# Attention and a gated block on one core: in the first four slots, where the weights' half-made words stand, when their passes come, and who copies block C

## The chip, the cores and the metric

The kernel runs on one core of one Trainium2 chip. The metric is the device time of one execution, in microseconds (us). Inputs are in the chip's main memory; the host only lays data out.

## The reference, cut to what matters

```python
# attention: q, k, v are (8, 8, 576, 64); blocks of 64 positions, block-causal mask
scores = (q @ k.T) / sqrt(64)                     # per batch and head
scores = where(block(i) >= block(j), scores, -1e9)
attn = exp(scores - max(scores))
attn = attn / (sum(attn) + 1e-9)
x = (attn @ v)                                    # heads joined: (8, 576, 512)
# gated block
h = gelu_tanh(x @ w_in)                           # w_in (512, 1024)
u, v = h[..., :512], h[..., 512:]
v_n = (v - mean(v)) / sqrt(var(v) + 1e-6) * g_ln  # over the last axis
v_s = w_sg @ v_n + b_sg                           # w_sg (576, 576), over positions
out = x + (u * v_s) @ w_out                       # w_out (512, 512)
```

w_in and w_out come as 64-bit floating-point words; everything else is 32-bit. The products keep nearly full 32-bit accuracy: each operand is split into a high and a low part (`hi`, `lo`) of a type that TensorE multiplies at speed, and three products are added up.

## The kernel before, in words

The attention is done for pairs of heads: 8 batches x 4 pairs = 32 pairs, one pair in one *slot* of the main loop (slots 0 to 31). Slots 0 to 3 are the first batch and run `opening_slot`; the others run `slot`, where pieces of the gated block of the batch before are put between the steps. This text is about slots 0 to 3.

A pair's 576 query rows are five blocks of rows: number 0 has 64 rows, numbers 1 to 4 have 128. Under the mask, block i has 64 + 128 i columns (64, 192, 320, 448, 576). Its work is spread over two slots. In slot n:

- TensorE turns the exponents of pair n (in `prob0` to `prob4`) by transposes, in five groups of four 128x128 tiles, each group in one PSUM bank: A0 and A1 (row block 4, first and second head), B0 and B1 (row blocks 3 and 1), C (row block 2, both heads). The banks are named `pA`, `pB`, `pC`; each is copied to SBUF into `ptA`, `ptB`, `ptC`. The table `TE` says which engine copies: ScalarE A0 and B0, VectorE A1, B1 and C.
- VectorE makes the inverse sums (`r`), ScalarE spreads them (`rx`).
- TensorE makes the first score products `s` of pair n+1 (row blocks 4, 1 and 0), then `turn_sums`: transposes of the diagonal blocks and of `rx` into banks `pd` and `pe`, which ScalarE copies to `rb`.
- VectorE adds the mask to the scores and takes their maxima in one custom instruction (`prob<-s,mask`, and a short one that reads the accumulator, `negm`): the *first maxima*. The one for row block 1 writes `prob1`, which the transposes for `pd` still read, and so waits for them. ScalarE then makes the exponents with their sums (`prob<-prob,negm`).
- `second` does the same for row blocks 3 and 2: the *second products, maxima and exponents*.
- `products`: TensorE multiplies the turned exponents by `v` into bank `ob` (a last piece goes to `pe`); `normalise`: VectorE multiplies `ob` by `rb` into `x`, which is spilled to memory. The high and low parts `xh` and `xl` are made in the next slot (`split_pending`).
- `split_qk`: GpSimd splits q and k of pair n+2 into `qh`, `ql`, `kh`, `kl`, one buffer each, so that it has to wait until the second products of pair n+1 have read the old ones.

The weights w_in come in 256 columns at a time and need work, since they are 64-bit words. `Double` takes a raw tile apart: ScalarE makes one word from the high halves (`m`), and three VectorE instructions, the *passes* of `single`, make the 32-bit number: one takes three bits from the low halves, one adds the sign, one adds `m`. The words `raw`, `m` and `t` all are in SBUF pages of the tag `w`. GpSimd then splits the number into `wi_h` and `wi_l` (`split_weight`). The generator `load_weight` gives these three steps one by one, and each call of `weight_half` takes one; the eight tiles of part "v" are treated three, two, two and one at a time in slots 0 to 3, and parts "u", "s" (the spatial matrix) and "o" come in later slots.

PSUM has eight banks, all of one pool (`bank`); a new tile takes a bank that its last user has left. Up to slot 3 VectorE, ScalarE and GpSimd do their instructions in the order in which the code writes them; from slot 4 on only TensorE does, and a scheduler places the others. Transfers are issued by SyncE in one queue: an issue that waits holds up those behind it.

Of the kernel before, what the change touches and what calls it, by code (L numbers as in the profile page):

```python
# [9 lines left out]
F32 = mybir.dt.float32  # L10
F32R = mybir.dt.float32r
BF16 = mybir.dt.bfloat16
U32 = mybir.dt.uint32
AF = mybir.ActivationFunctionType
ALU = mybir.AluOpType
# [5 lines left out]
def kernel(  # L21
# [13 lines left out]
    B, H, D, S = qT.shape  # L35
    P = 128
    BLK = 64
    DM = H * D
    DFF = w_in.shape[1]
    DH = DFF // 2  # L40
# [11 lines left out]
    class Engine:  # L52


        def __init__(self, letter, engine):
            self.letter, self.engine = letter, engine
# [5 lines left out]
    vector = Engine("V", nc.vector)  # L62
# [13 lines left out]
    def page(dtype, n, name):  # L76
        tag, bufs = KINDS.get(name, KINDS["w"])
        return sp.tile([P, n], dtype, tag=tag, name=name, bufs=bufs)

    def bank(name):  # L80
        return psum.tile([P, 512], F32, tag="bank", name=name, bufs=8)
# [7 lines left out]
    def turn(out, in_):  # L89
        return tensor.transpose(out, in_, ident)  # L90

    def copy(e, dst, src):
        f = {"v": vector.tensor_copy, "a": scalar.copy, "g": gpsimd.tensor_copy}[e]
        return f(dst, src)
# [3 lines left out]
    raw = {}  # L98
# [13 lines left out]
    def split_qk(n):  # L112
        out = []
        for x, t in zip(raw.pop(n), "qk"):
            hi = sp.tile([P, S], F32R, tag=t + "h", name=t + "h", bufs=1)
            lo = sp.tile([P, S], F32R, tag=t + "l", name=t + "l", bufs=1)
            if n == 0:
                copy("v" if t == "q" else "a", hi, x)
                vector.tensor_tensor(lo, x, hi.bitcast(F32), op=ALU.subtract)
            else:  # L120
                copy("g", hi, x)
                behind["G"] = gpsimd.tensor_tensor(lo, x, hi.bitcast(F32), op=ALU.subtract)
            out += [hi, lo]
        qk[n] = out

    def load_v(n):
        b, h = PAIRS[n]
        v_f, v_d = vals[n] = v_bufs[n % 2]
        lo, hi = slice(0, BLK), slice(BLK, P)
        for a, r in ((0, lo), (1, hi)):  # L130
            cols = slice((h + a) * D, (h + a + 1) * D)
            x = v[b, : (NT - 1) * P, cols].rearrange("(j p) d -> p j d", p=P)
            if a == 0:
                nc.sync.dma_start(v_f[:, :, r], x)
            else:
                nc.sync.dma_start(v_f[lo, :, r], x[hi])
                nc.sync.dma_start(v_f[hi, :, r], x[lo])
            nc.sync.dma_start(v_d[r, : NT - 1, r], x[lo])
            nc.sync.dma_start(v_d[r, NT - 1, r], v[b, S - TAIL :, cols])
# [24 lines left out]
    for s in (0, 1):  # L164
        t = cp.tile([P, NT - 1, 2 * D], F32, name=f"v_f{s}")
# [11 lines left out]
    wi_h = cp.tile([P, NC, DFF], F32R, name="wi_h")  # L177
    wi_l = cp.tile([P, NC, DFF], F32R, name="wi_l")
    wo_h = cp.tile([P, NC, DM], F32R, name="wo_h")
    wo_l = cp.tile([P, NC, DM], F32R, name="wo_l")  # L180
# [5 lines left out]
    def split_weight(x, dh, dl):  # L186
        gpsimd.tensor_copy(dh, x)
        gpsimd.tensor_tensor(dl, x, dh.bitcast(F32), op=ALU.subtract)

    class Double:  # L190


        def __init__(self, raw, name):
            n = raw.shape[-1]
            words = raw.bitcast(U32).rearrange("p (n t) -> p n t", t=2)
            self.hi, self.lo = words[:, :, 1], words[:, :, 0]
            tm = page(U32, 2 * n, name)
            self.t, self.m = tm[:, :n], tm[:, n:]
            scalar.activation(
                self.m.bitcast(F32), self.hi.bitcast(F32), AF.Abs, scale=2.0**-112  # L200
            )

        def single(self):
            t = self.t
            vector.tensor_scalar(t, self.lo, 29, None, op0=ALU.logical_shift_right)
            vector.scalar_tensor_tensor(
                t, self.hi, 0x80000000, t, op0=ALU.bitwise_and, op1=ALU.bitwise_or
            )
            vector.scalar_tensor_tensor(
                t, self.m, 3, t, op0=ALU.logical_shift_left, op1=ALU.bitwise_or  # L210
            )
            return t.bitcast(F32)

    def load_weight(src, cols, dh, dl, name="w", ahead=2, groups=()):

        W = 256
        parts = [(c, slice(f, f + W)) for f in range(cols.start, cols.stop, W) for c in range(NC)]
        raws = {}

        def fetch(k):  # L220
            if k < len(parts):
                c, fs = parts[k]
                raws[k] = page(src.dtype, W, name)
                nc.sync.dma_start(raws[k], src[c * P : (c + 1) * P, fs])

        for k in range(ahead):
            fetch(k)
        k = 0
        for size in (*groups, *([1] * len(parts))):
            if k == len(parts):  # L230
                return
            opened = []
            for j in range(k, k + size):
                fetch(j + ahead)
                raw = raws.pop(j)
                opened.append(raw if src.dtype == F32 else Double(raw, name))
            yield False
            if src.dtype != F32:
                opened = [x.single() for x in opened]
            yield False  # L240
            for j, x in zip(range(k, k + size), opened):
                c, fs = parts[j]
                split_weight(x, dh[:, c, fs], dl[:, c, fs])
            k += size
            yield True

    def load_spatial():
# [20 lines left out]
        for j in range(NT - 1):  # L268
# [15 lines left out]

    weights = deque(
        [
            ("v", load_weight(w_in, slice(DH, DFF), wi_h, wi_l, "w", 3, (3, 2, 2, 1))),
            ("u", load_weight(w_in, slice(0, DH), wi_h, wi_l)),
            ("s", load_spatial()),
            ("o", load_weight(w_out, slice(0, DM), wo_h, wo_l, "xr", 0)),  # L290
        ]
    )

    def weight_half():

        while weights:
            said = next(weights[0][1], None)
            if said is not None:
                return said
            weights.popleft()  # L300
# [16 lines left out]
    class Scores:  # L317
# [85 lines left out]
        def second(self):  # L403
            self.step((3, 0, EXT[3]))
            self.step((2, 0, EXT[2]))

    TE = {"A0": "a", "A1": "v", "B0": "a", "B1": "v", "C": "v"}
    PLACES = {
        "A0": [(0, 4, j) for j in range(4)],
# [6 lines left out]
    class Values:  # L416
# [9 lines left out]
        def turn(self, which):  # L426

            t = bank("p" + which)
            pt = sp.tile([P, 512], F32, tag="pt", name="pt" + which, bufs=5)
            for c, (a, i, j) in enumerate(PLACES[which]):  # L430
                c = slice(c * P, (c + 1) * P)
                k = BLK + P * (i - 1 - j) if a else P * j
                turn(t[:, c], prob[a][i][:, k : k + P])
                self.pt[a, i, j] = pt[:, c]
            copy(TE[which], pt, t)

        def inverse(self):

# [270 lines left out]
    def load_share(n, k):  # L709

        if n in WS:
            with ExitStack() as order:
                for ins in behind.values():
                    order.enter_context(tc.issue_after(ins.ins))
                for _ in range(WS[n][k]):
                    weight_step()

    PLAN = ["1112", "2114", "2114", "2114"]
    FIRST = ["1112", "1111", "1111", "2114"]
    Q = H // 2  # L720

    def split_pending():

        for f in pending:
            f()
        pending.clear()

    def opening_slot(n, va):

        va.turn("A0")  # L730
        va.turn("A1")
        va.turn("B0")
        va.turn("B1")
        va.inverse()
        split_pending()
        va.turn("C")
        load_v(n + 1)
        load_qk(n + 2)
        nx = Scores(n + 1)
        for p in nx.FIRST:  # L740
            nx.products(*p)
        va.turn_sums()
        weight_half()
        for p in nx.FIRST:
            nx.softmax(*p)
        weight_half()
        if n < Q - 1:
            nx.second()
            split_qk(n + 2)
            weight_half()  # L750
            va.products()
            va.normalise()
            pending.append(va.split)
        else:
            weight_half()
            va.products()
            va.normalise()
            va.split()
            nx.second()
        nv = Values(n + 1, nx)  # L760
        if n == Q - 1:
            nv.inverse()
            split_qk(n + 2)
        return nx, nv

    def slot(n, va):
        nx = n + 1 < N
        k = 6 if n // Q == 1 else 3
        g = [int(x) for x in (FIRST if n // Q == 1 else PLAN)[n % Q]]
        if n + 1 < N:  # L770
# [25 lines left out]
        load_share(n, 2)  # L796
        if n == Q + 1:
            run_side(2 * NT + 1)
        if n % Q == Q - 1:
            va.split()  # L800
# [81 lines left out]
```

## Time and profile before

| what | value |
|---|---|
| median of 3 runs | 758.80 us (758.28 to 758.92) |
| the profiled execution's own time | 758.84 us |
| its span in the profile | 757.0 us |
| mean granted TensorE clock | 0.993 |
| TensorE busy | 735.8 us (97%) |
| VectorE busy | 474.8 us (63%) |
| ScalarE busy | 425.3 us (56%) |
| GpSimd busy | 305.0 us (40%) |

The profile calls the engines PE (TensorE's matmuls and transposes), DVE (VectorE), ACT (ScalarE), POOL (GpSimd) and SP (SyncE, whose queue issues transfers). The span is from the first to the last instruction. Shares are means over the whole span: a stage with other limits has to be read by itself. In rows in order of time the first number is the start in us from the span's start and the second the length; a bracket gives the idle time of the engine just before and what ended it. A row that ends in "x2" stands for two instructions that follow each other. Line 60 is the helper that records nearly all instructions, so rows are told apart by the names of their tiles.

### The profile page before, as it was taken

To read this page: it belongs to the slowest core of one execution; us is meant where nothing else is said; L and a number is where in the kernel's file an instruction comes from. 1 tells how busy PE (TensorE), PEld (TensorE's weight loads), DVE (VectorE), ACT (ScalarE), POOL (GpSimd) and SP (SyncE) were. 2 spreads that over 40 slices of the span, in tenths; PEclk is the share of its full clock that TensorE was granted. 3 is DMA by queue.
4 is the path that set the end of the run, shared out by engine and by line. 5 is a ranking of instruction groups with operands and counts; after the bars stand their busy time and mean duration, and the time that the engine had idled before them with its cause. 6 is when DMAs were issued, how large, how long until landed. Compare 5 with 4: busy or idle time off the path is not lost.

```text
span 757.0 us, 18446 instructions
## 1 busy us (share of the span) xinstructions
PE 735.8 (97%) x6946; PEld 693.2 (92%) x6946; DVE 474.8 (63%) x1477; ACT 425.3 (56%) x1064; POOL 305.0 (40%) x376
## 2 busy tenths in 40 slices
PE   8779998999999999999999999999999999999998
PEld 7668998989899899999999899998999989998998
DVE  6988889765855359544785348664495645941732
ACT  5666767457744678337764377544873467721600
POOL 3755697634445323343433334351234532322121
PEclk9979999999999999999999999999999999999999
DMA  6626243333352223322234122521235221120032
GB/s 195 199 69 213 68 121 98 85 95 93 105 160 71 58 79 95 108 69 71 71 118 118 32 71 70 175 75 48 58 85 163 71 57 54 65 78 16 2 126 94
DMA packets 84300, 70.05 MB, mean 93 GB/s; under 512 B 59890, under 2 KB 59890, under 8 KB 84212
## 3 DMA queue, kind: packets, MB, share of 16 engines
q1 hardware_dynamic: 84212, 68.88, 31.0%
q8 instruction: 55, 0.90, 0.5%
q14 instruction: 33, 0.27, 0.1%
HBM read 49.98 MB, written 18.87 MB: 91 GB/s over the span
## 4 chain that ended last, share of the span: by engine, by line
PE 73%; DVE 8%; POOL 5%; DMA 5%; ACT 3%; issue 3%; SPq 2%; DVEq 0%; POOLq 0%; ACTq 0%
PE accs L60 16%; PE acco L60 11%; PE accv L60 11%; PE accu L60 9%; PE s L60 8%; PE ob L60 8%; PE pB L60 3%; PE pA L60 2%; PE pd L60 2%; DVE w L60 2%; ACT prob L60 2%; DVE prob L60 2%; DMA xr<-in_w_out 1%; PE pC L60 1%; POOL rs L60 1%
## 5 line engine op out<-in xcount | busy, mean ns | idle before, releaser
L60 ACT ACTIVATE prob<-prob,negm 128x576 f32<-128x576 f32 (+3 forms) x320 | 176.6, 554 | 70.1 <-DVE negm L60 68.9
L60 DVE CUSTOM_DVE_ANT_0 prob<-s,mask 128x256 f32<-128x256 f32 (+3 forms) x320 | 119.8, 418 | 44.9 <-PE s L60 41.6
L60 POOL TENSOR_TENSOR xh<-x,xh 128x64 fp32r<-128x64 f32 x32 | 10.8, 337 | 196.2 <-DVE xh L60 174.4
L60 POOL TENSOR_TENSOR gl<-u,gh 128x288 fp32r<-128x288 f32 x64 | 52.1, 819 | 88.7 <-DVE gh L60 72.8
L60 PE MATMUL acco<-gh,wo_h 128*128 128x288 f32 x256 | 77.6, 303 | 1.7 <-ACT ptB L60 1.4
L60 PE MATMUL accu<-xh,wi_h 128*128 128x288 f32 x256 | 78.3, 306 | 0.3 <-DVE negm L60 0.3
L60 PE MATMUL accs<-ws_h,vh 128*128 128x288 f32 x256 | 78.0, 305 | 0.0
L60 PE MATMUL accs<-ws_h,vl 128*128 128x288 f32 x256 | 75.5, 295 | 1.7 <-DVE vl L60 1.7
L60 PE MATMUL acco<-gl,wo_h 128*128 128x288 f32 x256 | 75.5, 295 | 0.0
L60 PE MATMUL accu<-xl,wi_h 128*128 128x288 f32 x256 | 75.5, 295 | 0.0
L60 PE MATMUL accs<-ws_l,vh 128*128 128x288 f32 x256 | 75.4, 295 | 0.0
L60 PE MATMUL accu<-xh,wi_l 128*128 128x288 f32 x256 | 75.3, 294 | 0.0
L60 PE MATMUL acco<-gh,wo_l 128*128 128x288 f32 x256 | 75.3, 294 | 0.0
L60 DVE TENSOR_TENSOR u<-accs,u 128x288 f32<-128x288 f32 x64 | 29.2, 457 | 58.3 <-PE accs L60 57.4
L60 PE MATMUL accv<-wi_h,xh 128*128 128x512 f32 x160 | 65.4, 409 | 0.0
L60 PE MATMUL s<-kh,qh 64*128 64x320 f32 (+4 forms) x384 | 64.2, 328 | 0.0
L60 PE MATMUL accv<-wi_l,xh 128*128 128x512 f32 x160 | 62.9, 393 | 0.0
L60 PE MATMUL s<-kh,ql 64*128 64x320 f32 (+4 forms) x384 | 59.8, 305 | 0.9 <-POOL ql L60 0.9
L60 ACT ACTIVATION_READ_ACCUMULATOR prob<-prob,negm 128x1 f32 x320 | 60.0, 188 | 0.0
L60 PE MATMUL s<-kl,qh 64*128 64x320 f32 (+4 forms) x384 | 58.8, 304 | 0.3 <-POOL kl L60 0.3
L60 ACT COPY vv<-accv 128x512 f32<-128x512 f32 x32 | 18.6, 581 | 65.6 <-PE accv L60 65.6
L60 PEld LDWEIGHTS acco<-gh,wo_h 128*128 128x128 f32 x256 | 48.1, 188 | 3.4 <-ACT ptB L60 1.8
(115 smaller groups left out, 2088.5 us busy)
## 6 DMA issues: line engine op xcount, KB each, us to landing
q_f<-in_qT SPq DMA_DIRECT2D x32, 288.0 KB, 3.1
k_f<-in_kT SPq DMA_DIRECT2D x32, 288.0 KB, 3.1
spill<-x SPq DMA_DIRECT2D x32, 288.0 KB, 2.7
xr<-spill SPq DMA_DIRECT2D x32, 288.0 KB, 3.0
out_T<-xr SPq DMA_DIRECT2D x32, 288.0 KB, 2.8
v_f<-in_v SPq DMA_DIRECT2D x32, 128.0 KB, 2.6
v_d<-in_v SPq DMA_DIRECT2D x64, 64.0 KB, 2.7
v_f<-in_v SPq DMA_DIRECT2D x64, 64.0 KB, 2.6
```

What stands on the lines that cost most here:

```text
L60: return lambda *a, **k: pin(method(*a, **k), self.letter)
```

## The change

Three edits, all in effect in slots 0 to 3 alone.

1. For part "v" the first two passes write their half-made word into a PSUM bank (`bank("w")`); the third reads it there and writes the finished number to SBUF.
2. In slots 0, 1 and 2 the call of `weight_half` that makes the passes moves behind `nx.second()`. Slot 3 keeps its order.
3. Block C of pairs 0 to 3 is copied by ScalarE.

```diff
     class Double:
-        def __init__(self, raw, name):
+        def __init__(self, raw, name, part):
             n = raw.shape[-1]
+            self.part = part
...
         def single(self):
-            t = self.t
-            vector.tensor_scalar(t, self.lo, 29, None, op0=ALU.logical_shift_right)
+            t = x = self.t
+            if self.part == "v":
+                x = bank("w").bitcast(U32)[:, : t.shape[-1]]
+            vector.tensor_scalar(x, self.lo, 29, None, op0=ALU.logical_shift_right)
             vector.scalar_tensor_tensor(
-                t, self.hi, 0x80000000, t, op0=ALU.bitwise_and, op1=ALU.bitwise_or
+                x, self.hi, 0x80000000, x, op0=ALU.bitwise_and, op1=ALU.bitwise_or
             )
             vector.scalar_tensor_tensor(
-                t, self.m, 3, t, op0=ALU.logical_shift_left, op1=ALU.bitwise_or
+                t, self.m, 3, x, op0=ALU.logical_shift_left, op1=ALU.bitwise_or
             )
...
+    Q = H // 2
     TE = {"A0": "a", "A1": "v", "B0": "a", "B1": "v", "C": "v"}
...
-            copy(TE[which], pt, t)
+            copy("a" if which == "C" and self.n < Q else TE[which], pt, t)
...
         for p in nx.FIRST:
             nx.softmax(*p)
-        weight_half()
         if n < Q - 1:
             nx.second()
+            weight_half()
             split_qk(n + 2)
             weight_half()
             va.products()
             va.normalise()
             pending.append(va.split)
         else:
+            weight_half()
             weight_half()
             va.products()
```

(The calls of `load_weight` pass the part's name.)

On VectorE, in slot 1, from the last of the first maxima (row block 0, 64x64) to the copy of A1, before:

```order
L60 ISA prob_110,negm<-s,mask 64x64
L60 ISA negm 64x1
L60 TENSOR_SCALAR w<-w 128x256
L60 SCALAR_TENSOR_TENSOR w<-w 128x256 x2
L60 TENSOR_SCALAR w<-w 128x256
L60 SCALAR_TENSOR_TENSOR w<-w 128x256 x2
L60 ISA prob_113,negm<-s,mask 128x448
L60 ISA negm 128x1
L60 ISA prob_113,negm<-s,mask 128x7x64
L60 ISA negm 128x1
```

and now:

```order
L60 ISA prob_113,negm<-s,mask 128x448
L60 ISA negm 128x1
L60 ISA prob_113,negm<-s,mask 128x7x64
L60 ISA negm 128x1
L60 ISA prob_112,negm<-s,mask 128x320
L60 ISA negm 128x1
L60 ISA prob_112,negm<-s,mask 128x5x64
L60 ISA negm 128x1
L60 TENSOR_SCALAR w<-w 128x256
L60 SCALAR_TENSOR_TENSOR w<-w 128x256 x2
L60 TENSOR_SCALAR w<-w 128x256
L60 SCALAR_TENSOR_TENSOR w<-w 128x256 x2
```

The two weights' passes (`w<-w`) stood ahead of the four second maxima (prob_113 is row block 3, prob_112 row block 2) and now stand behind them, ahead of normalise.

On ScalarE, from the copy of A0 to the weights' step, in slot 1 before:

```order
L60 COPY ptA_452<-pA_451 128x512
L60 COPY ptB_466<-pB_465 128x512
L60 COPY rx<-r 128x640
L60 COPY rb<-pd 128x512
L60 COPY rb<-pe 128x384
L60 ACTIVATE w<-w 128x256 x2
```

and now:

```order
L60 COPY ptA_455<-pA_454 128x512
L60 COPY ptB_469<-pB_468 128x512
L60 COPY rx<-r 128x640
L60 COPY ptC<-pC 128x512
L60 COPY rb<-pd 128x512
L60 COPY rb<-pe 128x384
L60 ACTIVATE w<-w 128x256 x2
```

The copy of block C came in, behind rx. On VectorE it is gone from behind `xh<-x`.

In SyncE's queue, the loads that are issued in slot 1 and 2 (pair 3's v, the spill, pair 4's q and k), before:

```order
L138 DMA v_d_107<-in_v 64x4x64
L490 DMA spill<-x 128x576
L136 DMA v_f_106<-in_v 64x4x64
L137 DMA v_f_106<-in_v 64x4x64
L138 DMA v_d_107<-in_v 64x4x64
L109 DMA k_f<-in_kT 128x576
```

and now:

```order
L227 DMA w<-in_w_in 128x256
L108 DMA q_f<-in_qT 128x576
L139 DMA v_d_107<-in_v 64x64 x2
L109 DMA k_f<-in_kT 128x576
L134 DMA v_f_106<-in_v 128x4x64
L138 DMA v_d_107<-in_v 64x4x64
L494 DMA spill<-x 128x576
L136 DMA v_f_106<-in_v 64x4x64
L137 DMA v_f_106<-in_v 64x4x64
L138 DMA v_d_107<-in_v 64x4x64
```

The loads of q and k stand ahead of most of the v loads and of the spill. TensorE's order is the same instruction by instruction through the whole program. From slot 4 on the scheduler changed little: in one place, near 120 us of the profile before, VectorE now makes all four low parts `vl` of the gated block ahead of a pair's normalise, where two stood behind it.

More of the change, by code (lines that the diff above doesn't have):

```diff
@@ L203, in single, with load_weight @@
         def single(self):
-            t = self.t
-            vector.tensor_scalar(t, self.lo, 29, None, op0=ALU.logical_shift_right)
+            t = x = self.t
+            if self.part == "v":
+                x = bank("w").bitcast(U32)[:, : t.shape[-1]]
+            vector.tensor_scalar(x, self.lo, 29, None, op0=ALU.logical_shift_right)
             vector.scalar_tensor_tensor(
-                t, self.hi, 0x80000000, t, op0=ALU.bitwise_and, op1=ALU.bitwise_or
+                x, self.hi, 0x80000000, x, op0=ALU.bitwise_and, op1=ALU.bitwise_or
             )
             vector.scalar_tensor_tensor(
-                t, self.m, 3, t, op0=ALU.logical_shift_left, op1=ALU.bitwise_or
+                t, self.m, 3, x, op0=ALU.logical_shift_left, op1=ALU.bitwise_or
             )
             return t.bitcast(F32)
-    def load_weight(src, cols, dh, dl, name="w", ahead=2, groups=()):
+    def load_weight(part, src, cols, dh, dl, name="w", ahead=2, groups=()):
         W = 256
@@ L235, in load_weight @@
                 raw = raws.pop(j)
-                opened.append(raw if src.dtype == F32 else Double(raw, name))
+                opened.append(raw if src.dtype == F32 else Double(raw, name, part))
             yield False
@@ L286 @@
         [
-            ("v", load_weight(w_in, slice(DH, DFF), wi_h, wi_l, "w", 3, (3, 2, 2, 1))),
-            ("u", load_weight(w_in, slice(0, DH), wi_h, wi_l)),
+            ("v", load_weight("v", w_in, slice(DH, DFF), wi_h, wi_l, "w", 3, (3, 2, 2, 1))),
+            ("u", load_weight("u", w_in, slice(0, DH), wi_h, wi_l)),
             ("s", load_spatial()),
-            ("o", load_weight(w_out, slice(0, DM), wo_h, wo_l, "xr", 0)),
+            ("o", load_weight("o", w_out, slice(0, DM), wo_h, wo_l, "xr", 0)),
         ]
@@ L719 @@
     FIRST = ["1112", "1111", "1111", "2114"]
-    Q = H // 2
     def split_pending():
```

## The prediction

> **What bounds the kernel now.** I read the page's head first, then the busy time by stage, then what TensorE waits for, the chain of waits, and last each engine's order of time in the first four slots. On the page:
>
> ```profile
> PE 735.8 (97%) x6946; PEld 693.2 (92%) x6946; DVE 474.8 (63%) x1477; ACT 425.3 (56%) x1064; POOL 305.0 (40%) x376
> ```
>
> TensorE sets the end. By stage (from:to, length, then busy us of PE, PEld, DVE, ACT, POOL, PE's clock, DMA share, GB/s):
>
> ```profile
> 24.20:39.10 14.90, 10.36 (x126) 8.63 (x126) 14.30 (x41) 8.86 (x28) 14.26 (x20) 0.96 0.48 137
> 39.10:54.30 15.20, 12.16 (x127) 11.07 (x127) 12.96 (x41) 8.92 (x28) 8.63 (x12) 0.81 0.27 73
> 140.00:757.00 617.00, 611.47 (x5659) 580.63 (x5657) 358.67 (x1121) 329.58 (x803) 215.79 (x253) 1.00 0.29 84
> ```
>
> Late in the span TensorE is 99% busy; in slots 1 and 2 it is not, while VectorE and GpSimd are nearly full. The waits of PE (total, times, longest; first row before 64 us, the others behind it), and from the chain of waits the rows of slot 1 (start, length):
>
> ```profile
> PE pB L60 <- ACT prob L60: 9.1, 4, 4.1
> PE accs L60 <- DVE vl L60: 1.7, 1, 1.7
> PE pA L60 <- ACT vh L60: 1.1, 1, 1.1
> ```
>
> ```profile
> 35.55 1.59 DVE w L60
> ...
> 38.30 0.50 ACT prob L60
> ...
> 39.12 1.97 PE pB L60 x8
> ```
>
> So in a slot TensorE's block B waits for exponents, these for the second maxima on VectorE, and these for the weights' passes that stand ahead of them. Behind 64 us hardly 4 us of waits are left: what the slots save, the end should gain.
>
> VectorE in order of time (start, length; the bracket is idle time and its releaser). The 128x192 maxima with a bracket, or first in their slot, are my mark T, where the diagonal's transposes let the first maxima go on:
>
> ```profile
> 16.54 0.36 DVE L60 CUSTOM_DVE_ANT_0 prob<-s,mask 128x192 f32<-128x192 f32 x1 [0.65 <-PE pd L60]
> ...
> 18.68 0.28 DVE L60 TENSOR_SCALAR w<-w 128x256 uint32<-128x256 uint32 x1
> ...
> 19.87 0.29 DVE L60 TENSOR_SCALAR w<-w 128x256 uint32<-128x256 uint32 x1
> ...
> 28.98 0.36 DVE L60 CUSTOM_DVE_ANT_0 prob<-s,mask 128x192 f32<-128x192 f32 x1 [0.29 <-PE pd L60]
> ...
> 31.11 1.38 DVE L60 TENSOR_SCALAR w<-w 128x256 uint32<-128x256 uint32 x1
> ...
> 37.59 0.61 DVE L60 CUSTOM_DVE_ANT_0 prob<-s,mask 128x448 f32<-128x448 f32 x1
> ...
> 39.50 0.68 DVE L60 TENSOR_TENSOR x<-ob,rb 128x512 f32<-128x512 f32 x1
> ...
> 41.12 0.69 DVE L60 COPY ptB<-pB 128x512 f32<-128x512 f32 x1 [0.22 <-PE pB L60]
> ...
> 42.38 0.68 DVE L60 COPY ptC<-pC 128x512 f32<-128x512 f32 x1
> ...
> 45.20 0.36 DVE L60 CUSTOM_DVE_ANT_0 prob<-s,mask 128x192 f32<-128x192 f32 x1 [1.27 <-PE pd L60]
> ...
> 47.34 0.28 DVE L60 TENSOR_SCALAR w<-w 128x256 uint32<-128x256 uint32 x1
> ...
> 59.57 0.36 DVE L60 CUSTOM_DVE_ANT_0 prob<-s,mask 128x192 f32<-128x192 f32 x1 [0.74 <-PE pd L60]
> ```
>
> T is 16.54, 28.98, 45.20 and 59.57 in slots 0 to 3. GpSimd beside it:
>
> ```profile
> 22.83 0.66 POOL L60 CAST qh<-q_f 128x576 fp32r<-128x576 f32 x1 [9.00 <-DMA q_f<-in_qT]
> ...
> 25.69 1.41 POOL L60 TENSOR_TENSOR kl<-k_f,kh 128x576 fp32r<-128x576 f32 x1
> ...
> 35.45 1.40 POOL L60 TENSOR_TENSOR kl<-k_f,kh 128x576 fp32r<-128x576 f32 x1
> ...
> 47.38 0.76 POOL L60 CAST qh<-q_f 128x576 fp32r<-128x576 f32 x1 [3.11 <-PE s L60]
> ```
>
> One weight's three passes take 1.19 us (18.68 to 19.87) while GpSimd idles, and 3.24 (31.11 to 37.59 for two weights) while it works. The maxima, which read one input from PSUM, take 2.13 from T to the passes beside a working GpSimd (28.98 to 31.11) and 2.14 beside an idle one (45.20 to 47.34). What slows an instruction under GpSimd is reading and writing SBUF alone.
>
> **The change, part by part.** Block C's copy first: it leaves VectorE (its 0.68 ahead of the first maxima) and goes into ScalarE's order behind rx, where ScalarE idles anyway until pd. ScalarE's rows:
>
> ```profile
> 23.41 0.67 ACT L60 ACTIVATE prob<-prob,negm 128x448 f32<-128x448 f32 x1 [1.31 <-DVE negm L60]
> ...
> 31.09 0.47 ACT L60 ACTIVATE prob<-prob,negm 128x192 f32<-128x192 f32 x1
> ...
> 34.06 0.19 ACT L60 ACTIVATION_READ_ACCUMULATOR prob<-prob,negm 64x1 f32 x1
> ...
> 45.80 0.59 ACT L60 COPY rb<-pd 128x512 f32<-128x512 f32 x1 [2.84 <-PE pd L60]
> ```
>
> Even the 0.68 of VectorE's copy lies within the 2.84 idle; in the short slots below it still fits, since ScalarE is busy under 9 of about 10 us (8.86 and 8.92 by stage, plus the copy). Cost: nothing.
>
> Passes in PSUM, per weight: the first loses its 0.28, a price seen here only from SBUF to SBUF, for the 0.42 of a 128x256 instruction with a PSUM side; the others stay at the median 0.43:
>
> ```profile
> L60 DVE CUSTOM_DVE_ANT_0 prob<-s,mask 128x256 f32<-128x256 f32 x10 | 4.2, 421 | 2.7 <-PE s L60 2.7
> ```
>
> ```profile
> L60 DVE SCALAR_TENSOR_TENSOR w<-w x32: 357/426/1577, 19.0 to 91.3; 128x256 uint32<-128x256 uint32 x32
> ```
>
> So 1.19 + 0.14 = 1.33 a weight. No row shows VectorE writing PSUM, so I bound it: 1.19 if nothing is lost, 3.24 if GpSimd is still in the way. I take 1.33, since the nearest row, the maxima with one side in PSUM, shows no slowing.
>
> Order: the second maxima now follow the first at T + 2.13 and take 1.91 (37.59 to 39.50); TensorE's products for them stand ahead already. Then passes, normalise, copies. The new round of a slot, first on the chain ScalarE-TensorE: the first exponents start at T + 2.11 (31.09) and end at T + 5.27 (34.06 + 0.19). They, no longer the maxima (T + 4.04), now release the second exponents. From the second exponents to the next products s, to pd and to the next T, slot 0 shows the steps at full clock:
>
> ```profile
> 14.49 0.39 PE L60 MATMUL s<-kh,qh 64*128 64x256 f32 x2
> ...
> 16.07 0.77 PE L60 MATMUL pd<-ident,prob 128*128 128x128 f32 x5
> ...
> 24.22 1.31 PE L60 MATMUL pB<-ident,prob 128*128 128x128 f32 x8 [1.66 <-ACT prob L60]
> ...
> 26.33 0.39 PE L60 MATMUL s<-kh,qh 64*128 64x256 f32 x2
> ...
> 27.15 0.39 PE L60 MATMUL s<-kl,qh 64*128 64x256 f32 x2 [0.31 <-POOL kl L60]
> ...
> 41.87 0.58 PE L60 MATMUL s<-kh,qh 64*128 64x256 f32 x2
> ...
> 44.73 0.76 PE L60 MATMUL pd<-ident,prob 128*128 128x128 f32 x5
> ```
>
> 23.41 to 26.33 is 2.92, 14.49 to 16.07 is 1.58, 16.07 to 16.54 is 0.47: round 5.27 + 2.92 + 1.58 + 0.47 = 10.24. VectorE's own round: 2.13 + 1.91 + 2 x 1.33 + 2.66 (39.50 to 42.38 less the 0.22 idle: normalise, two copies, r, xh; block C gone) + 0.42 (first maximum) = 9.78, just under. GpSimd starts its split of the next pair when the second products are done (47.38, T + 2.18) and needs 4.27 for it (22.83 to 27.10, kl's end): T + 6.45, and products s come at T + 5.27 + 2.92 = T + 8.19. So 10.24 is the round, and VectorE is next with 0.46 in hand.
>
> Slot 0 gains nothing: exponents come 1.3 us sooner, but products s wait for kl, whose chain starts when q_f lands (22.83), and kl ends at 27.10 as before. T of slot 1 stays 28.98. Then 39.22 instead of 45.20, and 49.46 instead of 59.57: 10.11 saved. The next kl, held up by GpSimd's queue of the start, ends at 36.85 or sooner; products s come at 28.98 + 8.19 = 37.17: no wait, by 0.3.
>
> The queue of SyncE changes too: the loads q_f and k_f of the next pair now stand ahead of the v loads and of the w load, which wait behind them for GpSimd's split. v is read a slot later, and the w load is the eighth weight's, used in slot 3: both have a slot to spare, so nothing. The w tiles take PSUM banks from the same eight. Each is free again after its weight's third pass, T + 4.04 + 2 x 1.33 = T + 6.70 at the latest; the tile ob is free after normalise's first instruction, 0.68 later, T + 7.4. The next user of these banks is a block of transposes or products s at T + 8.19, so nobody waits while the passes are cheap; at 3.24 a weight ob's bank would come at T + 11.2 and products s would wait for it. Slot 3 keeps its order: its one weight costs 0.14 more. Behind it everything is released by the slots' pace and moves along: 0, with VectorE's waits named above (1.7 and 1.1) as what may shrink or grow.
>
> Sum against the profiled execution: 758.84 - 10.11 + 0.14 = **748.9** (span 757.0; the median of the runs is 758.80, 0.04 off).
>
> **Rivals.**
> (1) The passes are slowed as before, since their raw words still come from SBUF. For it: the third pass writes SBUF. Against: the maxima, which write SBUF too. VectorE's round is then 7.12 + 6.48 = 13.60, T of slot 3 56.18, gain 3.4: 755.4. [...] Chance 8%, for the write into PSUM that no row shows.
> (2) TensorE's clock falls in the short slots, because in slot 0 it now waits for kl. Slot 2 shows the slow step: pB to s 2.75 (39.12 to 41.87) for 2.11 (24.22 to 26.33), s to pd 2.86 for 1.58. That is 1.92 a slot, 3.84 for two: 752.7. Against: slot 0's idle 1.66 left 26.33 and its followers at full pace, only the 4.1 in slot 1 did not; the new wait is shorter than 2. [...] Chance 10%.
> (3) The gain is given back between 64 and 125 us, where weights u and the spatial matrix come in by DMA and GpSimd. If the loads there kept their times, TensorE would wait. As much as the two slow steps of this kind that TensorE shows, 1.7 + 1.1, doubled: 5.6 back, 754.5. Against: those loads wait for pages that the slots free, so they come sooner too. Chance 8%.
> (4) Slower: VectorE's write into PSUM, beside TensorE's, is dear. The point from which it decides: the old rounds average (59.57 - 28.98) / 2 = 15.30, so two weights must cost 15.30 - 7.12 = 8.18, or 1.36 a pass. At the longest pass seen (1.577) the round is 7.12 + 9.46 = 16.58, T of slot 3 62.14: 761.4. Only passes under contention come near it. Chance 4%.
> That the change doesn't do what it says is rival 1.
>
> **How the numbers follow.** My forecast, 746 to 751.5, has 67%; the rivals 8, 10, 8 and 4; 3% is for no change by a cause I can't name. Low end 746: the waits for vl and vh (1.7 + 1.1) vanish, as all four vl now stand ahead of normalise in that slot (748.9 - 2.8 = 746.1). Passes at the middle of their bounds, 2.2 a weight, make VectorE's round 7.12 + 4.4 = 11.5, T of slot 3 52.0 and the gain 7.6: 751.4, the end of the forecast's own range. The range for 8 in 10 reaches on over rivals 2 and 3 to 754.5; outside stay rivals 1 and 4 and no change (15%), and a few per cent below 746. A measurement can tell 0.2% here, 1.5 us. Faster than that: 67 + 8 + 10 + 8 = 93; within it 3; slower 4.
>
> **What would show it.** Right: the mark T stands near 29, 39 and 49.5; passes at 0.4 to 0.45 each beside a busy GpSimd; the second exponents follow the first without idle time; PE's waits for prob fall from 9.1 to under 3; clock 1.00 from 24 to 50. Wrong: passes over 1 us (rival 1 or 4), s over 0.5 (rival 2), new PE waits between 50 and 115 (rival 3).

## The result, and the profile after

The changed kernel takes 752.98 us (median of 4 runs, 752.00 to 753.83) beside 758.54 for the kernel before (757.59 to 758.92): ratio 0.9928, interval 0.9911 to 0.9945. It is faster by 5.6 us, where 748.9 against 758.84 was forecast, a gain of 9.9. 752.98 lies outside 746 to 751.5, the forecast's own part of the range, and inside the whole range up to 754.5, which takes in rivals 2 and 3. The profiled execution took 752.41 us; its span is 750.6. Its busy time on the page:

```profile
PE 733.8 (98%) x6946; PEld 691.4 (92%) x6946; DVE 468.2 (62%) x1473; ACT 427.3 (57%) x1068; POOL 302.6 (40%) x376
```

By stage, with the columns of the table before (the last row is the same stretch up to the span's end, which now begins 6.4 us sooner):

```profile
24.20:39.10 14.90, 12.27 (x127) 10.89 (x125) 11.38 (x40) 9.16 (x29) 13.03 (x18) 0.77 0.47 133
39.10:54.30 15.20, 14.96 (x194) 13.06 (x196) 14.43 (x59) 13.09 (x38) 11.37 (x19) 1.00 0.57 155
133.60:750.60 617.00, 611.19 (x5657) 580.34 (x5655) 358.39 (x1119) 329.68 (x803) 215.23 (x252) 1.00 0.28 84
```

The stage of slots 2 and 3 is now full of TensorE work at full clock (14.96 of 15.20, before 12.16 at 0.81). The stage of slot 1 is not: its clock is 0.77. Behind 134 us nothing changed (611.19 busy, before 611.47). What PE waits for before 140 us:

```profile
PE pA L60 <- DVE x L60: 2.7, 1, 2.7
PE s L60 <- POOL ql L60: 1.8, 1, 1.8
PE warm L60 <- POOL ident masks.py:199: 1.8, 1, 1.8
PE s L60 <- DVE ptB L60: 1.6, 1, 1.6
PE s L60 <- POOL kl L60: 1.0, 1, 1.0
PE ob L60 <- DVE negm L60: 0.7, 1, 0.7
...
PE pB L60 <- ACT prob L60: 0.3, 1, 0.3
```

The wait of pB for exponents, 9.1 us before, is down to 0.3. VectorE's rows in order of time, the mark T of slots 0 to 3 among them, and the passes of slots 0 and 1:

```profile
15.99 0.36 DVE L60 CUSTOM_DVE_ANT_0 prob<-s,mask 128x192 f32<-128x192 f32 x1 [0.65 <-PE pd L60]
...
20.04 0.41 DVE L60 TENSOR_SCALAR w<-w 128x256 uint32<-128x256 uint32 x1
20.49 0.97 DVE L60 SCALAR_TENSOR_TENSOR w<-w 128x256 uint32<-128x256 uint32 x2
21.38 0.42 DVE L60 TENSOR_SCALAR w<-w 128x256 uint32<-128x256 uint32 x1
...
30.70 0.36 DVE L60 CUSTOM_DVE_ANT_0 prob<-s,mask 128x192 f32<-128x192 f32 x1 [1.52 <-PE pd L60]
...
33.66 0.63 DVE L60 CUSTOM_DVE_ANT_0 prob<-s,mask 128x448 f32<-128x448 f32 x1 [0.74 <-PE s L60]
...
35.58 0.44 DVE L60 TENSOR_SCALAR w<-w 128x256 uint32<-128x256 uint32 x1
36.05 0.95 DVE L60 SCALAR_TENSOR_TENSOR w<-w 128x256 uint32<-128x256 uint32 x2
36.92 0.42 DVE L60 TENSOR_SCALAR w<-w 128x256 uint32<-128x256 uint32 x1
...
41.60 0.35 DVE L60 CUSTOM_DVE_ANT_0 prob<-s,mask 128x192 f32<-128x192 f32 x1
...
51.91 0.36 DVE L60 CUSTOM_DVE_ANT_0 prob<-s,mask 128x192 f32<-128x192 f32 x1 [0.43 <-PE pd L60]
```

One weight's passes take 1.34 us (20.04 to 21.38, 35.58 to 36.92), in slot 1 beside a GpSimd that works. T is 15.99, 30.70, 41.60 and 51.91: slot 3 begins 7.66 us sooner than before, not 10.11. Most of what is missing went in slot 1. GpSimd's split, TensorE's rows, and the clock in stretches of 2 us there:

```profile
23.25 0.66 POOL L60 CAST qh<-q_f 128x576 fp32r<-128x576 f32 x1 [9.45 <-DMA q_f<-in_qT]
...
26.09 1.40 POOL L60 TENSOR_TENSOR kl<-k_f,kh 128x576 fp32r<-128x576 f32 x1
```

```profile
26.06 0.38 PE L60 MATMUL s<-kh,qh 64*128 64x256 f32 x2 [1.65 <-DVE ptB L60]
...
27.55 0.58 PE L60 MATMUL s<-kl,qh 64*128 64x256 f32 x2 [0.98 <-POOL kl L60]
...
29.98 1.33 PE L60 MATMUL pd<-ident,prob 128*128 128x128 f32 x5
```

```profile
24.00:26.00 2.00, 0.41 (x2) 0.17 (x2) 2.00 (x6) 0.87 (x2) 2.00 (x2) 1.00 0.16 52
26.00:28.00 2.00, 0.96 (x8) 0.75 (x10) 1.77 (x4) 1.21 (x2) 1.92 (x3) 0.62 0.57 149
28.00:30.00 2.00, 2.00 (x21) 1.94 (x19) 0.43 (x2) 0.00 (x0) 1.84 (x5) 0.50 0.45 109
30.00:32.00 2.00, 2.00 (x12) 1.97 (x10) 1.30 (x7) 0.17 (x1) 1.92 (x5) 0.50 0.90 279
32.00:34.00 2.00, 2.00 (x15) 1.40 (x14) 1.25 (x9) 2.00 (x7) 0.85 (x2) 0.67 0.50 125
```

TensorE has turned blocks A to C early and waits for the split, 1.65 and 0.98 us (the first bracket names VectorE's copy ptB, which ends together with GpSimd's kh; in e5 below the same products start at 25.25, right behind kh's end of 25.21 and before that copy begins at 25.34, so it is kh that holds them). Then the clock is 0.50 until about 33.3: from kl's end (27.49) to T it takes 3.21 us, where the kernel before needed 1.88 (27.10 to 28.98), and pd takes 1.33 instead of 0.77.

### The profile page after: what moved, and what is told of

Same layout as the page of the kernel before. It is cut to its first block, busy times and chain, and to the rows that moved or that the text cites. A ratio compares the mean times of both kernels' runs of the same rounds, so it can differ in the third digit from the quotient of the medians.

```text
span 750.6 us, 18464 instructions
## 1 busy us (share of the span) xinstructions
PE 733.8 (98%) x6946; PEld 691.4 (92%) x6946; DVE 468.2 (62%) x1473; ACT 427.3 (57%) x1068; POOL 302.6 (40%) x376
## 4 chain that ended last, share of the span: by engine, by line
PE 77%; DVE 7%; DMA 5%; ACT 5%; POOL 3%; SPq 2%; issue 2%; DVEq 0%; ACTq 0%; POOLq 0%
PE accs L60 15%; PE accv L60 12%; PE acco L60 11%; PE accu L60 10%; PE s L60 9%; PE ob L60 9%; PE pd L60 3%; PE pB L60 3%; PE pA L60 3%; ACT prob L60 2%; DVE prob L60 2%; DMA xr<-in_w_out 2%; PE pe L60 1%; POOL rs L60 1%; PE pC L60 1%
```

## The experiments

e1 to e4 were timed together, beside 757.66 us for the kernel before (755.05 to 760.62); e5 to e8 together at another time, beside 757.65 (755.55 to 759.41).

| run | us | ratio to before, interval | T of slots 1, 2, 3 |
|---|---|---|---|
| e1: order alone | 754.25 | 0.9955, 0.9938 to 0.9972 | 30.23, 43.77, 55.50 |
| e2: PSUM words alone | 750.78 | 0.9904, 0.9883 to 0.9926 | 29.11, 39.62, 50.14 |
| e3: changed, C on VectorE | 751.58 | 0.9924, 0.9901 to 0.9948 | 30.71, 42.13, 52.34 |
| e4: changed, early loads of q, k | 749.63 | 0.9899, 0.9877 to 0.9921 | 26.84, 37.15, 47.23 |
| e5: changed, again | 753.05 | 0.9938, 0.9918 to 0.9958 | 29.89, 40.86, 50.98 |
| e6: changed, old order | 750.19 | 0.9903, 0.9885 to 0.9922 | 29.61, 40.11, 50.61 |
| e7: changed, transposes in the gap | 749.88 | 0.9901, 0.9881 to 0.9922 | 28.37, 38.51, 48.64 |
| e8: e6 with early loads | 749.06 | 0.9886, 0.9866 to 0.9906 | 28.27, 38.78, 49.28 |

**e1, the order alone.** The kernel before, with the passes behind the second maxima in slots 0 to 2:

```diff
-        weight_half()
         if n < Q - 1:
             nx.second()
+            weight_half()
...
         else:
+            weight_half()
             weight_half()
```

> Only the order of the changed kernel: the passes stand behind the second maxima in slots 0 to 2, but stay in SBUF, and VectorE copies block C. Theory (GpSimd slows the passes, and that is most of the gain): a weight still costs 2.7 to 3.2 us in slots 1 and 2, VectorE's round is 7.12 + 6 + 0.6 = 13.7, T of slot 3 lies near 57.5 to 58.5 and the time near 756.5 to 757.5. Rival (the order is the gain, the passes' length is hidden): as the changed kernel, 752 to 754.

Measured 754.25: 3.4 us of gain, more than expected. It lies between the theory (756.5 to 757.5) and the rival (752 to 754), so neither is met: with slow passes the order alone brings more than half of the change's gain. The passes in slot 1:

```profile
35.27 1.11 DVE L60 TENSOR_SCALAR w<-w 128x256 uint32<-128x256 uint32 x1
36.41 2.32 DVE L60 SCALAR_TENSOR_TENSOR w<-w 128x256 uint32<-128x256 uint32 x2
38.66 0.28 DVE L60 TENSOR_SCALAR w<-w 128x256 uint32<-128x256 uint32 x1
38.98 1.36 DVE L60 SCALAR_TENSOR_TENSOR w<-w 128x256 uint32<-128x256 uint32 x2
```

They are still slow beside GpSimd (3.39 for the first weight), but come later: GpSimd ends its split of q and k at 38.46 and then waits for weights itself, and the second weight takes 1.60 (38.66 to 40.26). The rounds are 13.54 and 11.73, before 16.22 and 14.37. In slot 1 the clock falls as in the changed kernel, from 26.82 to 33.64, and T is again 3.21 behind kl's end (27.02).

**e2, the PSUM words alone.** The first edit of the diff, the order and block C as before.

> Only the PSUM words: order and block C's copy as before. Theory (the passes' length is the gain): the second maxima come at T + 2.13 + 2.7, the second exponents could start at T + 5.4 instead of T + 5.27, so a round is at most 0.6 longer than in the changed kernel (block C's copy on VectorE); time 753 to 754.5. Rival (the order carries half or more): 755.5 to 757.

Measured 750.78, below both expectations (753 to 754.5 and 755.5 to 757). T of slots 1 to 3:

```profile
29.11 0.36 DVE L60 CUSTOM_DVE_ANT_0 prob<-s,mask 128x192 f32<-128x192 f32 x1 [0.27 <-PE pd L60]
...
39.62 0.36 DVE L60 CUSTOM_DVE_ANT_0 prob<-s,mask 128x192 f32<-128x192 f32 x1 [0.17 <-PE pd L60]
...
50.14 0.35 DVE L60 CUSTOM_DVE_ANT_0 prob<-s,mask 128x192 f32<-128x192 f32 x1
```

Rounds of 10.51 and 10.52 with the old order: the words in PSUM alone bring the whole gain, and slot 1 loses nothing to the clock, which is 1.00 from 24 to 46 us.

**e3, block C back on VectorE.**

```diff
-            copy("a" if which == "C" and self.n < Q else TE[which], pt, t)
+            copy(TE[which], pt, t)
```

> The changed kernel with block C copied by VectorE again. VectorE had no idle time in slot 1 and 0.43 us in slot 2 of the changed kernel, so 0.6 a slot lengthens two rounds by 0.2 to 0.6 each: 753.2 to 754.2. Rival (block C's copy costs nothing anywhere): 752.5 to 753.

Measured 751.58, below both expectations (753.2 to 754.2 and 752.5 to 753), beside 752.98 and 753.05 for the changed kernel at other times. T of slot 3 is 0.43 later in the profile, but the time is not longer: who copies C makes no difference that these runs can tell. The clock falls here too, from 26.34 to 33.17, and T of slot 1 is 3.21 behind kl's end (27.50).

**e4, early loads.** The changed kernel; the first two tiles of the spatial matrix and g_ln are issued behind the loads of q and k of pair 2.

```diff
-        nc.sync.dma_start(k_f, ...)
+        first_qk[n] = nc.sync.dma_start(k_f, ...)
...
+            with tc.issue_after(first_qk[2].ins):
+                return fetch_now(j)
...
+        with tc.issue_after(first_qk[2].ins):
+            nc.sync.dma_start(g_bc, ...)
```

> The changed kernel, with the loads of q and k of pair 2 issued ahead of the first two tiles of the spatial matrix and of g_ln (832 KB). Theory (slot 1 is late because q_f lands late, and its waiting lets TensorE's clock fall): kl is ready before the products ask for it, the clock stays at 1.00 from 24 to 34 us, T of slot 1 falls from 30.7 to 26.5 to 27.5, T of slot 3 from 51.9 to 47.5 to 48.5, time 748.5 to 750. Rival (another engine holds slot 1, or the gain is given back in the later loads): 751.5 to 753.

Measured 749.63. The split starts when q_f has landed, 2.75 us sooner than in the changed kernel:

```profile
20.50 0.66 POOL L60 CAST qh<-q_f 128x576 fp32r<-128x576 f32 x1 [6.74 <-DMA q_f<-in_qT]
```

kl no longer holds up slot 1 (T 26.84), the clock stays at 1.00 from 24 to 46 us, and the rounds are 10.31 and 10.08. T of slot 3 is 4.7 us sooner than in the changed kernel's first profile, the time 3.4 less by medians that were not taken side by side. Later, from 103.79 to 107.20, the clock falls once.

**e5, the changed kernel again**, without an edit.

> The changed kernel itself, beside the next three, so that they can be compared with it under the same conditions. Expected 752.0 to 753.8 us, a ratio of 0.991 to 0.9945, T of slots 1 to 3 at 30.7, 41.6 and 51.9, and a granted clock of 0.50 for some microseconds behind 28 us.

Measured 753.05 (750.84 to 754.18). GpSimd began its split sooner in this profile (22.43), and T of slot 1 is 29.89; still it comes 3.21 behind kl's end (26.68), at half clock. And here the clock fell a second time, within the wait of pA that the first profile shows up to 116.27 without a fall:

```profile
116.04 1.09 PE L60 MATMUL pA<-ident,prob 128*128 128x128 f32 x4 [3.23 <-DVE x L60]
```

The clock at the edges of both falls:

```profile
26.40:26.80 0.40, 0.06 (x2) 0.06 (x2) 0.36 (x2) 0.00 (x0) 0.40 (x2) 0.53 0.58 188
33.20:33.60 0.40, 0.40 (x8) 0.21 (x6) 0.40 (x3) 0.40 (x3) 0.00 (x0) 0.94 0.58 179
114.80:115.20 0.40, 0.00 (x0) 0.00 (x0) 0.40 (x1) 0.00 (x0) 0.00 (x0) 0.96 0.00 0
121.60:122.00 0.40, 0.40 (x4) 0.40 (x3) 0.36 (x2) 0.40 (x2) 0.40 (x2) 0.51 0.00 0
```

**e6, the old order.** The changed kernel with its second edit undone in slots 0 to 2:

```diff
         if n < Q - 1:
-            nx.second()
             weight_half()
+            nx.second()
```

> The change without its second edit: the words stand in PSUM and ScalarE copies block C, but the passes stay ahead of the second maxima. Theory A (with the passes at 1.33 a weight the order is worth nothing, and the new order only draws TensorE's work together, so that an idle stretch behind it lets the clock fall): clock 1.00 from 24 to 50, T of slot 1 at 29.1, rounds of 10.2 to 10.5, T of slot 3 at 49.6 to 50.1, and 1 to 2 us less time than the changed kernel, 750 to 751.5. Theory B (my prediction's working: the second maxima must come ahead of the passes for a round of 10.24): rounds of 12.0 or more, T of slot 3 at 53 or later, 754 or more.

Measured 750.19: 2.6 us less than e5 beside it (mean of six runs each; 95% interval 1.0 to 4.3). Theory A holds in time and clock, though T of slots 1 and 3 (29.61, 50.61) is 0.5 later than it had. VectorE and ScalarE in slot 1:

```profile
33.54 0.95 DVE L60 SCALAR_TENSOR_TENSOR w<-w 128x256 uint32<-128x256 uint32 x2
34.41 0.62 DVE L60 CUSTOM_DVE_ANT_0 prob<-s,mask 128x448 f32<-128x448 f32 x1
```

```profile
35.13 0.68 ACT L60 ACTIVATE prob<-prob,negm 128x448 f32<-128x448 f32 x1 [0.25 <-DVE negm L60]
```

With passes at 1.33 the second exponents wait only 0.25 us for their maxima although the passes stand ahead of these: rounds 10.50. What the order takes away elsewhere is in TensorE's work. The transposes of blocks A to C come later (C's start at 24.91, in the changed kernel at 23.59), and the wait before kh is 0.41 instead of 1.65; that before kl is 0.98 in both. PE is busy 1.79 and 0.70 us of 24:26 and 26:28 and the clock stays at 1.00. From kl's end (27.74) to T it takes 1.87. The moment alone hardly spared this execution, by an estimate from e5: its two falls are 88.75 apart, and 88.75 ahead of the fall at 115.15 here lies 26.40, where the changed kernel falls (26.48, in e5 26.42). In the 3.41 us up to there (half a fall of e5) TensorE is busy for 2.79 here, and for 1.76 and 1.87 in those two. Only near 115 us, behind a wait of pA of 2.9, does the clock fall here:

```profile
114.80:115.20 0.40, 0.40 (x5) 0.40 (x4) 0.40 (x3) 0.00 (x0) 0.00 (x0) 0.94 0.84 334
118.40:118.80 0.40, 0.40 (x4) 0.40 (x3) 0.40 (x2) 0.38 (x3) 0.40 (x1) 0.79 0.00 0
```

**e7, transposes in the gap.**

```diff
         va.turn("C")
+        if n == 1:
+            warm(bank("warm"), 14)
```

> The changed kernel with 14 transposes of the unit matrix (about 1.6 us of work whose result is not used) on TensorE in slot 1, behind block C's transposes, where TensorE waits 1.65 us for kh. Theory A (the loss in slot 1 is the clock that falls in the wait for kh and kl): the clock stays at 1.00 from 24 to 36, products s, pd and the first maximum follow kl's end of 27.5 at full pace, T of slot 1 at 29.3 to 29.5 instead of 30.70, slot 2's round 10.3 instead of 10.90, T of slot 3 at 49.8 to 50.2, and 1.2 to 2 us less time than the changed kernel. Theory B (the loss is kl's late end alone, and the clock only a sign): T of slot 1 stays within 0.3 of 30.7 and the time within 0.5 us.

Measured 749.88: 2.4 us less than e5 (interval 0.6 to 4.2), by work that is thrown away.

```profile
24.69 1.69 PE L60 MATMUL warm<-ident 128*128 128x128 f32 x14
26.32 0.39 PE L60 MATMUL s<-kh,qh 64*128 64x256 f32 x2
...
27.89 0.77 PE L60 MATMUL pd<-ident,prob 128*128 128x128 f32 x5
```

The clock is 1.00 from 24 to 46 us, T of slot 1 comes 2.00 behind kl's end (26.37, early in this execution, which is why T is 28.37 and not 29.4), and the rounds are 10.14 and 10.13. Theory A holds; the interval takes in the 1.2 to 2 us that it had. In this profile the clock still falls later, from 112.50 to 119.33, in a wait of pA of 3.33. The granted clock of all six runs is 0.995 to 0.997, in e5 0.991 to 0.995, in e6 0.995 to 1.000. Against e6, where the clock holds in these slots as well, the new order's rounds are 0.36 shorter: that is what the order is worth while the clock stays up, some 0.7 us for two rounds by the profiles. The times of e6 and e7, 0.2 us apart with an interval of 1.6 either way, can't tell it.

**e8, old order and early loads.** e6 with the edit of e4.

> The kernel of the run before last (words in PSUM, block C on ScalarE, old order), and the loads of q and k of pair 2 issued ahead of the first two tiles of the spatial matrix and of g_ln. Theory A: T of slot 1 at 26.5 to 27.5 as in the run with early loads, rounds of 10.3 to 10.6, T of slot 3 at 47.5 to 48.5, clock 1.00; with some 1 to 2 us given back between 60 and 120 us where TensorE waits for ql, x and rx: 748 to 750. Theory B (the gain of slots 1 to 3 is given back in full there, since GpSimd's and the loads' work of that stage sets its end): within 0.7 us of the run with the old order alone.

Measured 749.06, the lowest of all: 3.9 us less than e5 (interval 2.1 to 5.8), a version faster than both kernels. Against e6 it is 1.3 less with an interval of 1.7 either way, so what the early loads add to the old order stays open; T of slot 1, at 28.27, did not reach the expected 26.5 to 27.5. With early loads the new order of e4 is ahead at T (26.84 and 47.23 in slots 1 and 3, here 28.27 and 49.28), but its time of 749.63 is not lower. In its profile the clock is 1.00 also from 100 to 120 us, where pA waits only 0.7.

## Why the prediction was right or wrong

**Passes in PSUM: right.** Forecast 1.33 a weight, measured 1.34, at 0.41 to 0.48 an instruction beside a busy GpSimd. Rivals 1 and 4 are out. In e1, where the words stay in SBUF, the first round is 13.54, where rival 1 had worked out 13.60; that they are so close is luck. Two weights' passes took 4.99 there (35.27 to 40.26) and not 6.48; a wait of 0.91 for products at half clock and 0.60 for block C, which VectorE copies there, make up for it. The first pass had only one SBUF input before too, and took 1.38 beside GpSimd (31.11, during the split xl), where it takes 0.44 now (35.58) and 0.41 in e6 in the old order, during the same split (31.75): for it, the place of its output makes the difference. By what an output in SBUF is slowed, no run here shows.

**The round: right in slot 2, wrong in slot 1.** Forecast 10.24; slot 2 to 3 measured 10.31, e7 10.14 and 10.13. In both the second exponents follow the first without idle time, as forecast. Slot 1 to 2 took 10.90: the clock is at half until 33.3, and the second maxima wait 0.74 for products (33.66).

**"T of slot 1 stays 28.98": the step that failed.** It is 30.70. Of the 1.72, 0.39 is kl's end, 27.49 for 27.10, as q_f landed later in this execution (GpSimd began with it at 23.25; in the other runs without early loads between 22.10 and 23.49, so this is scatter). The other 1.33 is the clock, 3.21 for 1.88 from kl's end to T. This is rival 2, to which I gave 10%: its cause, the wait for kl in slot 0's stretch, was named rightly, but I priced it as a fall in two slots (3.84) and held it unlikely, since the earlier idle 1.66 had left the clock up and "only the 4.1 in slot 1 did not". That reading was wrong. The profile before shows the slow step in slot 2 as well, behind a wait of 3.02:

```profile
54.26 1.72 PE L60 MATMUL pB<-ident,prob 128*128 128x128 f32 x8 [3.02 <-ACT prob L60]
...
56.76 0.58 PE L60 MATMUL s<-kh,qh 64*128 64x256 f32 x2
```

There the clock is at half from 55.00 to 58.42, and the fall in slot 1 came at 37.94, when the wait of 4.1 had lasted only 2.95. In the changed kernel the loss came in one place, for 1.33 + 0.66 = 1.99 us, and e6 and e7 show it by taking it away in two ways, 2.6 and 2.4 us, with two medians of 750.19 and 749.88. A fall at 26.3 to 26.8, with T of slot 1 3.21 behind kl's end, stands in all four profiles with the new order and neither early loads nor filler work (the changed kernel, e1, e3, e5), and in none of the three with the old order and the old loads (before, e2, e6: 1.87 or 1.88). That the measured 752.98 lies beside rival 2's 752.7 is luck: that sum has 3.84 for the clock and nothing for what comes behind slot 3. The clock fell here with a longest wait of 1.65, as long as the 1.66 of the profile before behind which it stayed at 1.00 (24 to 28 us).

**Order: given a gain that it hardly has.** The sentence that the exponents, "no longer the maxima", release the second exponents is true, but I didn't price it by itself. By e6 it is the 0.25 that ScalarE waits, and 0.36 a round against e7. The whole gain stands in e2. The same order brings block C's transposes forward (23.59, in e6 24.91), so that TensorE stands still behind them for 1.65 until kh is there, and the clock falls at 26.48; with a wait of 0.41 (e6) or 1.69 us of transposes in the gap (e7) it stays at 1.00 there. In e1, with slow passes, the order does bring 3.4 us, although the clock falls there too.

**Block C: right.** No time to be seen by e3.

**"Behind it 0": wrong by 1.1.** The lead of 7.66 at slot 3 is 6.4 at the span's end; 0.14 of the 1.26 was forecast. 0.9 of it is GpSimd's ql near 105 us, for which PE now waits 1.80 instead of 0.90. GpSimd's two steps there, now and before:

```profile
100.57 3.26 POOL L60 CAST ws_h<-xr 128x576 fp32r<-128x576 f32 x1 [0.65 <-DMA xr<-in_w_sgT]
103.80 1.84 POOL L60 TENSOR_TENSOR ql<-q_f,qh 128x576 fp32r<-128x576 f32 x1
```

```profile
107.58 0.67 POOL L60 CAST ws_h<-xr 128x576 fp32r<-128x576 f32 x1
108.25 4.08 POOL L60 TENSOR_TENSOR ql<-q_f,qh 128x576 fp32r<-128x576 f32 x1
```

Each time one of the two is slow, the one that meets VectorE's work on vv, which begins at 100.61 now and began at 108.36 before: now the split of the spatial matrix (3.26 instead of 0.67), before ql (4.08 instead of 1.84). Together they take 5.07 and took 4.75, so only 0.3 of the loss is in them. The rest is the 0.65 that GpSimd now waits for the load of xr ahead of them, where it didn't wait before. What slows a step beside vv wasn't tried. The two waits of before near 121 and 125 us (1.12 + 1.69) became one, for x, of 2.67. So rival 3 holds in a small part, through a load that did not come sooner by as much as the slots. The hopes behind the low end, that the waits for vl and vh vanish, are not met.

**The sum.** 2.45 at T of slot 3 (0.39 + 1.33 + 0.66 + 0.07 in the last round) and 1.12 behind it make 3.57; the profiled execution's 752.41 is 3.5 above 748.9. The scatter of the runs is wider than before's spread shown at first (750.8 to 754.2 in e5); the clock's second fall, present in e5's profile and absent in the first, is one reason: from pA to the next pair's pd it takes 2.7 us longer in e5 (116.04 to 126.07) than in the first profile (116.27 to 123.61).

## What to carry to other kernels

Price each part of a change by itself from the same rows: here one part carries the gain, and one that sounded like its complement costs 2 us through the clock. Before moving a late engine's work, ask how much of a few microseconds the clocked engine will then stand still: here a stretch of 3.41 us with 1.65 of idle time cost 1.99 us behind it, more than the wait itself, and with 1.69 us of filler work (e7) or an earlier load for the wait's cause (e4) the clock stayed at 1.00 there. And where VectorE's instructions are slow beside a working GpSimd, try one of their operands in PSUM: here a weight's passes went from 3.24 to 1.34 us, although the first takes 0.41 there and 0.28 from SBUF to SBUF beside an idle GpSimd.

## What the runs showed of the hardware

- The clock can fall without a long empty stretch ahead of it. In the first profile it falls at 26.48, when in the 3.41 us before (half the length of the longer falls, next point) TensorE had been busy for 1.76 and had stood still for 1.65; in e5 at 26.42, with waits of 0.88 and about 0.7 in that time. In the first profile the wait of pA (113.60 to 116.27) puts 1.62 us of idle time into the stretch from 111.81 to 115.22, which begins 25 times 3.413 us (a 26th of e5's 88.75, next point) behind 26.48, and the clock stays at 1.00. The ten profiles hold eleven falls ahead of the end of TensorE's work; in the 3.41 us ahead of each TensorE is busy for 0.47 to 1.87 us, and for 1.79 in that stretch without a fall. So how much idle time makes the clock fall, these runs don't show.
- The falls last 6.8 us or half of that (e6: 115.15 to 118.57, by its two rows). Half it is in the four falls behind which TensorE worked through the first 3.41 us without a gap (before at 55.00, e3 at 118.50, e4 at 103.79, e6 at 115.15); in the seven others it was busy for 2.05 to 3.16 of these, and the fall lasted twice as long. In e5 the rows above give, by their shares of half clock, falls from 26.42 to 33.25 and from 115.17 to 121.99: 6.83 and 6.82 long, and 88.75 apart, which is 26.0 times half of 6.83. The two other profiles with two falls have spacings near whole multiples of that half too: 37.94 and 55.00 before are 17.06 or 5.0 halves apart, 26.34 and 118.50 in e3 92.16 or 27.0. From these three I estimate that it also matters where a wait lies, so that one of much the same length costs clock in one execution and none in the next; more than three spacings and the wait of pA, with a fall in e5 (3.23) and without one in the first profile (2.67), the runs don't show.
- VectorE writes PSUM, while TensorE writes PSUM too, at 0.41 to 0.44 us for the first pass's 128x256 words, whether GpSimd works (0.44 at 35.58, 0.42 at 36.92) or not (0.41 at 20.04, 0.42 at 21.38); from SBUF to SBUF, before, the same instruction takes 0.28 beside an idle GpSimd (18.68) and up to 1.38 beside a working one (31.11).
